# A written order for each engine's queue, from chunk 2 of a fused attention and two-layer MoE kernel on

## The chip, the cores and the metric

The kernel runs on 1 core of one Trainium2 chip. The metric is device time in microseconds of one execution, here the median of several runs. TensorE, VectorE (DVE), ScalarE (ACT), GpSimd (POOL) and SyncE (SP, which issues nearly all loads and stores) each work through a queue of their own in order, and wait for each other by semaphores.

## The reference

Three layers follow one another. Everything is float32 on the chip.

```
# 1. delta-rule attention, 4 batches x 8 heads, 768 positions, head size 48
for t in range(S):
    y[t]  = q[t] @ state
    v_old = state.T @ k_n[t]
    state = state + beta[t] * outer(k_n[t], v[t] - v_old)
# 2. dense layer on the 3072 tokens x 384
h = x @ w_in;  x = silu(h) @ w_out          # 384 -> 2048 -> 384
# 3. eight experts, one chosen per token, tokens with x @ w_skip <= 0 pass through
e = argmax(x @ w_gate);  out = x + p[e] * (relu(x @ w1[e]) @ w2[e])
```

## The kernel before, in words

The 768 positions are cut into 12 chunks (NCH) of 64. In a chunk the recurrence is written with matrices: the Gram matrix of the chunk's keys (grams) gives a triangular matrix that has to be inverted (`inverse(c)`, some 80 small steps in a row on VectorE, most of them the pairs of lines 457 and 462), and with the inverse and the state St the outputs and the next state follow. One chunk of one batch goes through these stages (`chain(c, b)`):

- `pre`: GpSimd scales the values into vp (line 512) and the inverse into T (line 518); ScalarE copies the state into SU (line 527).
- `ks` (line 534): state times keys, subtracted from vp by VectorE (line 542).
- `u1` (line 547): first half of the solution; ScalarE copies it into U (line 552), GpSimd into SU (line 556).
- `g21u` (line 564), subtracted on VectorE; `u2` (line 573), copied by ScalarE into SU (line 578).
- `supd` (line 591): the new state, copied into St by VectorE (line 594).
- `yout` (line 605): the output; ScalarE writes its high part into x (line 614) and VectorE the low part. After the last batch a small DMA on SyncE moves rows inside x (line 620).

Chunks are prepared two ahead in eight slots: SyncE loads kq (`load_qk`, line 140, four buffers) and PQ (line 1025), ScalarE spreads the keys into KtB (`prep_t`, line 295), TensorE makes the grams (`prep_g`, line 300), ScalarE takes the diagonal blocks into Gd (line 376) and the lower ones into G21 (line 342), and VectorE masks the gram into PQ (`mask_q`, line 354). The inverse reads Gd by two transposes (line 398) and ends with a scaling and a transpose into Xb (lines 477 and 479). Gd, the inverse's buffers and Xb exist once, for chunk 2 and later ones.

Layer 2 of chunk c has 256 tokens and goes in 16 SiLU tiles (MF) of 128 hidden units. `l1(c, m)` (line 631) is nine matmuls into a PSUM tile hp: weights and activations are split into a high and a low part, and three products of 3 matmuls each are added. ScalarE applies SiLU twice, into gh and gf (lines 636, 637), GpSimd takes the difference gl (line 638), and `l2` (line 648) is nine matmuls that add into xp. After tile 15, `x2out` copies xp (line 662 on VectorE, line 657 on ScalarE), six float32 matmuls (line 668, twelve records in the trace) transpose it and make the router's logits, ScalarE and VectorE take them out (lines 670, 673), SyncE stores rows of x2 and out (lines 678, 679). `route1` and `route2` choose the experts on VectorE (lines 693 to 756) and GpSimd scatters the token numbers (line 760); line 756 writes these numbers into ids. A matmul of float32 operands makes two records in the trace, one of l1 or l2 makes one.

What sets the order: the program gives each instruction a priority, by the `rank` under which it was written (a chunk's step, and within it CHAIN, PREP, INV, CONV, MOE in this order). A planner that knows an estimate of each duration goes through a simulated time and appends to each engine's queue the ready instruction of the best rank. Buffers are given out in the same order. So the queues hold chain, inverse, preparation and SiLU layer mixed as the planner saw them become ready. In the queues of before the SiLU layer of chunk c-1 runs beside the attention of chunk c and part of c+1.

The start of the program converts the dense layer's weights, on VectorE, up to 139 us. After the layer of chunk 11 come its routing, the gathers and the eight experts.

Of the kernel before, what the change touches and what calls it, by code (L numbers as in the profile page):

```python
# [8 lines left out]
F32 = mybir.dt.float32  # L9
# [7 lines left out]
AX = mybir.AxisListType  # L17
PSUM = bass.MemoryType.PSUM
DRAM = bass.MemoryType.DRAM


@with_exitstack
def kernel(
# [22 lines left out]

    nc = tc.nc
    NCH, B, _, _, NP, CH = qk.shape  # L50
    D = ki.shape[-1]
    H, S = 2 * NP, NCH * CH
# [234 lines left out]
    def slot(c, b):  # L287
        return slots[c * B + b]
# [78 lines left out]
        spread(j, kq_t[c, b][:, 1])  # L367

    def prep_g(c, b):
        j = slot(c, b)  # L370
        g = ps_g.tile([128, NP, 128], F32, tag="g", name="g")
        for p in range(NP):
            gram(j, p, g[:, p, :], kq_t[c, b][:, :, p, :])
        for blk in range(2):
            sl = slice(64 * blk, 64 * blk + 64)
            nc.scalar.activation(
                out=Gd[sl, b * NP:(b + 1) * NP, :], in_=g[sl, :, CH + 32 * blk:CH + 32 * blk + 32], func=AF.Copy
            )
        lower(j, g[:, :, CH:])
        mask_q(j, g[:, :, 0:CH])  # L380
# [7 lines left out]
    def inverse(c):  # L388

        steps = []  # L390
        V = nc.vector
        nw = ar.tile([128, 5, 32], F32, tag="nw", name="nw")
        Gi, X = (Gi1, X1) if c == 1 else ([Gi0[:, 0:16], Gi0[:, 16:32]], X0)
        tmp = tmps[c == 1]
        w = [nw[:, z, :] for z in range(5)]

        def fwd(y0):
            return V.transpose(
                out=Gi[y0 // 16],
                in_=Gd[:, :, y0:y0 + 16].rearrange("p i y -> p y i")[:, :, None, :].to_broadcast([128, 16, 2, 16]),  # L400
            )

        steps.append(lambda: fwd(0))
        steps.append(lambda: fwd(16))

        i0, i1 = w[0].bitcast(I32), w[1].bitcast(I32)

        def norm():
            if c < 2:
                nc.scalar.activation(out=X, in_=Xi, func=AF.Copy)  # L410
            else:
                nc.gpsimd.tensor_copy(out=X, in_=Xi)
            for z in range(2):
                i = V.tensor_scalar(
                    out=w[0][:, 16 * z:16 * z + 16],
                    in0=Gi[z].rearrange("p a b -> p (a b)")[:, 16 * z:512:33], scalar1=1e-30, scalar2=None,
                    op0=ALU.max,
                )
            return i

        steps.append(norm)
        steps.append(lambda: V.tensor_scalar(
            out=i1, in0=i0, scalar1=1, scalar2=None, op0=ALU.logical_shift_right))
        steps.append(lambda: V.tensor_scalar(
            out=i1, in0=i1, scalar1=-1.0, scalar2=float(0x5F3759DF), op0=ALU.mult, op1=ALU.add))
        for _ in range(3):
            steps.append(lambda: V.tensor_tensor(out=w[2], in0=w[1], in1=w[1], op=ALU.mult))
            steps.append(lambda: V.scalar_tensor_tensor(
                out=w[2], in0=w[2], scalar=-0.5, in1=w[0], op0=ALU.mult, op1=ALU.mult))
            steps.append(lambda: V.scalar_tensor_tensor(  # L430
                out=w[1], in0=w[2], scalar=1.5, in1=w[1], op0=ALU.add, op1=ALU.mult))
        steps.append(lambda: V.tensor_tensor(out=w[2], in0=w[1], in1=w[0], op=ALU.mult))
        steps.append(lambda: V.tensor_scalar(out=w[2], in0=w[2], scalar1=1e-6, scalar2=None, op0=ALU.add))
        steps.append(lambda: V.reciprocal(out=w[3], in_=w[2]))
        steps.append(lambda: V.tensor_tensor(out=w[4], in0=w[3], in1=bet[:, c, :], op=ALU.mult))
        steps.append(lambda: V.tensor_tensor(out=w[4], in0=w[4], in1=w[3], op=ALU.mult))

        E = nc.gpsimd if c == 1 else V
        pre = E is nc.gpsimd

        def scale(y0):
            return (nc.gpsimd if c else V).tensor_tensor(
                out=Gi[y0 // 16], in0=Gi[y0 // 16],
                in1=w[4][:, y0:y0 + 16, None].to_broadcast([128, 16, 32]), op=ALU.mult,
            )

        def flat(j, r0, r1):
            f = (r0 - j // 2) * j
            return tmp[:, f:f + (r1 - r0) * j].rearrange("p (n j) -> p n j", j=j)

        def mul(j, r0, r1):
            n = r1 - r0
            a = X[:, r0:r1, j:j + 1].to_broadcast([128, n, j])
            b = Gi[j // 16][:, j % 16:j % 16 + 1, 0:j].to_broadcast([128, n, j])
            if pre:
                return E.tensor_tensor(out=flat(j, r0, r1), in0=a, in1=b, op=ALU.mult)
            return V.scalar_tensor_tensor(  # L457
                out=flat(j, r0, r1), in0=a, scalar=w[4][:, j:j + 1], in1=b, op0=ALU.mult, op1=ALU.mult
            )

        def sub(j, r0, r1):
            return E.tensor_tensor(  # L462
                out=X[:, r0:r1, 0:j], in0=X[:, r0:r1, 0:j], in1=flat(j, r0, r1), op=ALU.subtract
            )

        if pre:
            steps.append(lambda: scale(16))
        for j in range(31, 0, -1):
            if pre and j == 28:
                steps.append(lambda: scale(0))  # L470
            r0 = j // 2
            for f in (mul, sub):
                steps.append(lambda f=f, j=j, r0=r0: f(j, r0, 16))

        def last():
            V.transpose(out=nat, in_=w[2])
            V.tensor_tensor(
                out=X, in0=X, in1=w[4][:, None, :].to_broadcast([128, 16, 32]), op=ALU.mult)
            return V.transpose(out=Xb.rearrange("p i (r s) -> p r s i", s=2), in_=X)

        pace["inv", c] = [i for i in (f() for f in steps) if i is not None]
        return last

# [23 lines left out]
        return dict(vp=vp, T=T, U=U, su=su, pr=ru[:, 0], pu=ru[:, 1])  # L507

    def pre(c, b):
        g = gr[c, b] = tiles(c, b)  # L510
        vp, T, su = g["vp"], g["T"], g["su"]
        nc.gpsimd.tensor_tensor(
            out=vp,
            in0=v_t[c, b // 2][:, b % 2 * NP:(b % 2 + 1) * NP],
            in1=nat[:, b * NP:(b + 1) * NP][:, :, None].to_broadcast([128, NP, D]),
            op=ALU.mult,
        )
        nc.gpsimd.tensor_tensor(
            out=T,
            in0=Xb[:, b * NP:(b + 1) * NP, None, :].to_broadcast([128, NP, 2, 32]),  # L520
            in1=m2[:, None, :, None].to_broadcast([128, NP, 2, 32]),
            op=ALU.mult,
        )
        if c:
            with tc.issue_after(seen["hi", 0].ins) if c == 1 else ExitStack():
                for h, _, n, r0, r1 in feat:
                    nc.scalar.activation(out=su[r0:r0 + n, h, :, 0:D], in_=St[r1:r1 + n, b], func=AF.Copy)  # L527

    def ks(c, b):
        g = gr[c, b]  # L530
# [65 lines left out]
    def yout(c, b):  # L596
        g = gr[c, b]
        j = slot(c, b)
        if c or b % 2 == 0:
            py = ps_c.tile([128, NP, CH], F32, tag="y", name="py", bufs=1)  # L600
        else:
            py = ps_g.tile([128, NP, CH], F32, tag="g", name="py")
# [400 lines left out]
            tc.cur_priority = self.old  # L1003

    marks = {}
    js1 = []
    gates = deque()
    todo = deque(range(NCH * B))
# [2 lines left out]
    def prep():  # L1011
        while free and todo:
# [3 lines left out]
            with rank(c - 1, PREP):  # L1016
                if c == 0 and b == B - 1:
                    prep_0()
                elif c:
# [9 lines left out]
                    elif b == B - 1:  # L1029
                        js1[:] = [slot(c, i) for i in range(B)]  # L1030
                        grams(c, js1, 1)
            if b == B - 1 and c:
                with rank(c - 1, INV) if c > 1 else rank(0, INV):
                    last_of[c] = inverse(c)
            if b == B - 1 and not c:
# [2 lines left out]
    def chain(c, b):  # L1038
        with rank(c, CHAIN):
            with rank(c, CHAIN) if c else rank(-2, 5 + b):  # L1040
                if b % 2 == 0:
                    load_v(c, b // 2, nc.sync)
                if c < NCH - 1:
                    load_k(c, b, nc.sync)
            pre(c, b)
        if b == B - 1 and 0 < c < NCH - 1:
            with rank(c, INV):
                last_of.pop(c + 1)()
        with rank(c, CHAIN):
            with tc.issue_after(seen["yout", 0].ins) if c == 1 else ExitStack():  # L1050
                ks(c, b)
            u1(c, b)
            g21u(c, b)
            u2(c, b)
            if c:
                supd(c, b)
            yout(c, b)
            if not c:
                supd(c, b)
        free.append(slots[c * B + b])  # L1060
# [20 lines left out]
    def moe(c):  # L1081
        for m in range(MF + 1):
            moe_part(c, m)

    with rank(-2, 0):
        for z in (1, 0):
# [60 lines left out]
    for m in range(MF + 1):  # L1147
        moe_part(0, m)
    prep()
    for c in range(1, NCH):  # L1150
        for b in range(B):
            chain(c, b)
            prep()
        if c > 1:
            moe(c - 1)
    tc.cur_priority = (NCH + 2) * STEP + MOE
    st_att.close()
    open_e1()
# [135 lines left out]
```

## Time and profile before

| | us |
|---|---|
| median of 3 runs | 990.09 |
| lowest and highest run | 985.07, 994.03 |
| the profiled execution | 981.84 |
| its span, first to last instruction | 980.0 |

| engine | busy us in the span | share |
|---|---|---|
| TensorE matmul | 866.6 | 88% |
| VectorE | 607.8 | 62% |
| ScalarE | 476.1 | 49% |
| GpSimd | 398.0 | 41% |

Busy is the union of the instructions' times on an engine; for matmuls the end is modelled and holds the drain, under which the next matmul runs. The granted clock says at what share of 2.4 GHz TensorE was let run. Stretches below are cut at the first l1 matmul of a layer: the layer of chunk 1 begins at 148.7 us, the following ones at 224.1, 280.8, 346.0, 415.2, 481.4, 542.0, 597.3, 654.9 and 708.9, and that of chunk 11 at 758.0.

### The profile page before, as it was taken

How to read it: one execution, taken by the hardware profiler on the slowest of the kernel's cores; microseconds unless marked ns; L12 is line 12 of the kernel's file. 1: busy time of each engine (PE TensorE's matmuls, PEld its weight loads, DVE VectorE, ACT ScalarE, POOL GpSimd, SP SyncE). 2: the span in 40 equal slices, each digit the busy share in tenths (PEclk: the TensorE clock that was granted, in tenths of full speed). 3: DMA queues.
4: the chain of work that ended last, by engine and by line, in shares of the span. 5: the costliest groups of instructions: out<-in, count | busy, mean ns of one | idle time of the engine just before them, and what ended most of it. 6: DMA issues, size and time to landing. Idle time of an engine off the chain costs nothing. (4 is left out here: it accounts for less than half of the span.)

```text
span 980.0 us, 21718 instructions
## 1 busy us (share of the span) xinstructions
PE 866.6 (88%) x8177; PEld 827.5 (84%) x8177; DVE 607.8 (62%) x1776; ACT 476.1 (49%) x1290; POOL 398.0 (41%) x581
## 2 busy tenths in 40 slices
PE   7188998899996997978999999999999975999994
PEld 7177888889996987968999999899998964999994
DVE  5997999778624857357576954748523114776541
ACT  4167883465462553453464555445255342565520
POOL 4588663333322332422433342343345433435411
PEclk8567899998997997998999999999999996999998
DMA  9952221232222222132141222201018103866400
GB/s 306 401 172 73 69 77 43 59 87 77 69 65 77 63 71 83 31 108 58 46 123 30 86 73 74 82 12 47 9 35 267 34 17 107 283 202 204 151 20 23
DMA packets 64899, 95.83 MB, mean 98 GB/s; under 512 B 9290, under 2 KB 46232, under 8 KB 64784
## 3 DMA queue, kind: packets, MB, share of 16 engines
q1 hardware_dynamic: 61968, 89.69, 29.6%
q0 software_dynamic: 2816, 4.65, 1.7%
q8 instruction: 66, 1.08, 0.5%
q14 instruction: 49, 0.40, 0.1%
HBM read 80.79 MB, written 12.91 MB: 96 GB/s over the span
## 5 line engine op out<-in xcount | busy, mean ns | idle before, releaser
L631 PE MATMUL hp<-x,w 128*128 128x256 f32 x1728 | 263.6, 289 | 0.8 <-ACT gf L637 0.5
L638 POOL TENSOR_TENSOR gl<-gf,gh 128x256 fp32r<-128x256 f32 x192 | 147.8, 770 | 263.4 <-ACT gf L637 226.0
L631 PEld LDWEIGHTS hp<-x,w 128*128 128x128 f32 x1728 | 230.7, 194 | 3.1 <-ACT gf L637 0.7
L648 PE MATMUL xp<-gh,w 128*128 128x256 f32 x1152 | 184.2, 293 | 10.7 <-ACT gh L636 10.2
L648 PEld LDWEIGHTS xp<-gh,w 128*128 128x128 f32 x1152 | 154.5, 192 | 14.0 <-ACT gh L636 10.8
L636 ACT ACTIVATE gh<-hp 128x256 fp32r<-128x256 f32 x192 | 73.3, 382 | 176.9 <-PE hp L631 173.6
L457 DVE SCALAR_TENSOR_TENSOR tmp<-X,nw,Gi 128x126 f32<-128x126 f32 (+22 forms) x341 | 125.7, 369 | 9.3
L462 DVE TENSOR_TENSOR X<-X,tmp 128x126 f32<-128x126 f32 (+22 forms) x341 | 109.2, 320 | 8.8
L648 PE MATMUL xp<-gl,w 128*128 128x256 f32 x576 | 107.4, 293 | 3.4 <-POOL gl L638 3.3
L648 PEld LDWEIGHTS xp<-gl,w 128*128 128x128 f32 x576 | 83.5, 192 | 5.9 <-POOL gl L638 4.4
L527 ACT ACTIVATE SU<-St 32x192 f32<-32x192 f32 (+1 forms) x176 | 63.6, 361 | 46.5 <-PE py L605 22.4
L637 ACT ACTIVATE gf<-hp 128x256 f32<-128x256 f32 x192 | 72.9, 379 | 18.9 <-POOL gl L638 18.1
L300 PE MATMUL g<-kq,KtB 128*128 128x128 f32 (+1 forms) x384 | 66.1, 310 | 16.0 <-issue 10.2
L300 PEld LDWEIGHTS g<-kq,KtB 128*128 128x128 f32 x384 | 55.9, 215 | 18.4 <-issue 12.9
L881 PE MATMUL ehp<-exh,ew 128*128 128x256 f32 x384 | 66.8, 284 | 0.0
L814 ACT ACTIVATE ew<-eraw 128x768 fp32r<-128x768 f32 x64 | 53.3, 842 | 21.6 <-PE yp L903 15.4
L385 DVE TENSOR_TENSOR vp<-vp,ru 64x192 f32<-64x192 f32 x48 | 16.9, 358 | 75.0 <-PE ru L564 45.9
L816 DVE TENSOR_TENSOR ew<-eraw,ew 128x768 fp32r<-128x768 f32 x48 | 49.4, 1037 | 19.0 <-ACT ew L814 18.9
L354 DVE COPY_PREDICATED PQ<-mU,g 128x512 f32<-128x512 uint8 x44 | 31.9, 729 | 46.5 <-DMA PQ<-in_qp_dram 23.0
L881 PEld LDWEIGHTS ehp<-exh,ew 128*128 128x128 f32 x384 | 58.7, 191 | 0.0
L903 PE MATMUL yp<-ew,egh 128*128 128x384 f32 x256 | 57.4, 341 | 1.2 <-ACT egh L887 1.2
L534 PE MATMUL ru<-St,KtB 128*128 128x48 f32 x352 | 50.8, 279 | 5.2 <-DVE St L594 5.1
(170 smaller groups left out, 1458.5 us busy)
## 6 DMA issues: line engine op xcount, KB each, us to landing
eraw<-in_w_dram SPq DMA_DIRECT2D x64, 384.0 KB
kq<-in_qk_dram SPq DMA_DIRECT2D x44, 256.0 KB
PQ<-in_qp_dram SPq DMA_DIRECT2D x44, 256.0 KB
ki<-in_ki_dram SPq DMA_DIRECT2D x44, 192.0 KB
raw<-in_w_out_dram SPq DMA_DIRECT2D x16, 384.0 KB
raw<-in_w_in_dram SPq DMA_DIRECT2D x16, 384.0 KB
x2s<-xs SPq DMA_DIRECT2D x24, 197.0 KB
v<-in_v_dram SPq DMA_DIRECT2D x24, 192.0 KB
```

The source lines that it names most:

```text
L300: return nc.tensor.matmul(out, lhsT=KtB[j][:, p].rearrange("p k h t -> p (k h t)"), rhs=rhs, start=True, stop=True, skip_group_check=True,)
L457: return V.scalar_tensor_tensor(out=flat(j, r0, r1), in0=a, scalar=w[4][:, j:j + 1], in1=b, op0=ALU.mult, op1=ALU.mult)
L462: return E.tensor_tensor(out=X[:, r0:r1, 0:j], in0=X[:, r0:r1, 0:j], in1=flat(j, r0, r1), op=ALU.subtract)
L527: nc.scalar.activation(out=su[r0:r0 + n, h, :, 0:D], in_=St[r1:r1 + n, b], func=AF.Copy)
L631: nc.tensor.matmul(hp, lhsT=win[m][:, z, kk], rhs=x[:, kk, :], start=(n == 0), stop=(n == 8))
L636: nc.scalar.activation(out=gh, in_=hp, func=AF.Silu)
L637: nc.scalar.activation(out=gf, in_=hp, func=AF.Silu)
L638: (nc.vector if c == 0 and m in () else nc.gpsimd).tensor_tensor(out=gl, in0=gf, in1=gh.bitcast(F32), op=ALU.subtract)
L648: nc.tensor.matmul(mm[c][jj // 2][:, jj % 2], lhsT=wout[m][:, z, jj], rhs=g_, start=(m == 0 and g_ is gh and z == 0 and jj % 2 == 0), stop ...
L814: nc.scalar.activation(out=t[:, 0], in_=r, func=AF.Copy)
L881: i = nc.tensor.matmul(hp, lhsT=a[:, z, kk, fs], rhs=x[:, kk, :], start=(n == 0), stop=(n == 8))
L903: i = nc.tensor.matmul(ex["y", e][a], lhsT=g_[:, ts], rhs=b[:, z, m % mp], start=(m == 0 and n == 0), stop=(m == ME - 1 and n == 2),)
```

## The change

For chunks 2 to 11 the ranks no longer decide. A wrapper InOrder stands for the object that issues instructions; while it is on, it ties each instruction to the one written before it on the same engine. This is an edge for the planner alone: no semaphore and no instruction comes of it. A function `period(c)` writes the order: 17 steps m, each with l1 of tile m and l2 of tile m-1 of chunk c-1, one stage of the attention of chunk c for two batches (batches 0 and 1 in steps 0 to 4, 2 and 3 in steps 5 to 9), and steps of the inverse of chunk c+1 on VectorE, two at the step's beginning, one after each batch, two at its end. Loads, the routing of chunk c-2 and the preparation of chunk c+2 have fixed steps. `prep_g` and `pre` are cut in two so that their halves can be placed; in a period the odd batches' grams go into a PSUM tile of ps_c and the odd outputs into ps_g. Chunks 0 and 1, the preparation of chunk 3 and all after chunk 11's attention stay with the ranks.

```diff
+class InOrder:
...
+            def call(*args, **kw):
+                traced = own.tc.nc.cur_bb.bb.instructions
+                n = len(traced)
+                r = f(*args, **kw)
+                for i in traced[n:] if own.on else ():
+                    if i.engine in own.last:
+                        own.tc.add_manual_dep(
+                            i, own.last[i.engine],
+                            mybir.DependencyInfo(mybir.DependencyClass.NoSync, mybir.DependencyReason.DATA),
+                            reason="in order",
+                        )
+                    own.last[i.engine] = i.name
+                return r
...
-    nc = tc.nc
+    nc = InOrder(tc)
...
+    def prep_m(c, b):
         j = slot(c, b)
-        g = ps_g.tile([128, NP, 128], F32, tag="g", name="g")
+        if nc.on and b % 2:
+            g = ps_c.tile([128, NP, 128], F32, tag="c", name="g", bufs=2)
+        else:
+            g = ps_g.tile([128, NP, 128], F32, tag="g", name="g")
         for p in range(NP):
             gram(j, p, g[:, p, :], kq_t[c, b][:, :, p, :])
...
+        if nc.on:
+            return steps + [last]
         pace["inv", c] = [i for i in (f() for f in steps) if i is not None]
...
-        if c or b % 2 == 0:
+        if b % 2 == 0 or c and not nc.on:
             py = ps_c.tile([128, NP, CH], F32, tag="y", name="py", bufs=1)
...
-            if b == B - 1 and c:
+            if b == B - 1 and 0 < c < FIRST + 1:
...
+    def period(c):
+        more = c + 2 < NCH
+        inv = deque(inverse(c + 1) if c + 1 < NCH else ())
+        if c == FIRST:
+            for i in range(2):
+                load_v(c, i, nc.sync)
+                load_k(c, i, nc.sync)
+            for b in (0, 1):
+                pre_s(c, b, SU[b % 2])
+                pre_t(c, b)
+
+        def step(n):
+            for _ in range(n):
+                if len(inv) > 1:
+                    inv.popleft()()
+
+        def stage(f, bs):
+            for b in bs:
+                f(c, b)
+                step(1)
+
+        A, Z = (0, 1), (2, 3)
+        for m in range(MF + 1):
+            step(2)
+            if m < MF:
+                l1(c - 1, m)
+            if m:
+                l2(c - 1, m - 1)
+            if m < 4:
+                stage((ks, u1, g21u, u2)[m], A)
+            elif m == 4 or m == 9:
+                bs = A if m == 4 else Z
+                for f in (supd, yout):
+                    stage(f, bs)
+                for b in bs:
+                    if more:
+                        j = slots[(c + 2) * B + b] = slot(c, b)
+                        nc.sync.dma_start(out=PQ[j], in_=qp[c + 2, b])
+                    if m == 4 and c < NCH - 1:
+                        load_k(c, b + 2, nc.sync)
+                    if m == 9 and c < NCH - 2:
+                        load_k(c + 1, b - 2, nc.sync)
+                if m == 4:
+                    for b in Z:
+                        pre_t(c, b)
+            elif m < 9:
+                stage((ks, u1, g21u, u2)[m - 5], Z)
+            if m == 0:
+                finish(c - 2, 0)
+            elif m in (1, 3):
+                finish(c - 2, (m + 1) // 2)
+            if m in (0, 3) and more:
+                for b in ((0, 1) if m == 0 else (2, 3)):
+                    load_qk(c + 2, b, nc.sync)
+            if m in (1, 6) and c + 1 < NCH:
+                load_v(c + 1, m // 6, nc.sync)
+            if m in (5, 6):
+                pre_s(c, m - 3, SU[m % 2 ^ 1])
+            if m in (11, 12) and c + 1 < NCH:
+                pre_s(c + 1, m - 11, SU[m - 11])
+            if more:
+                if 6 <= m < 10:
+                    slots[(c + 2) * B + m - 6] = slot(c, m - 6)
+                    prep_t(c + 2, m - 6)
+                if m in (10, 13):
+                    b = (m - 10) // 3 * 2
+                    prep_m(c + 2, b)
+                    prep_m(c + 2, b + 1)
+                    prep_e(c + 2, b)
+                if m in (11, 14):
+                    prep_e(c + 2, (m - 11) // 3 * 2 + 1)
+            step(2)
+            if m == MF - 2:
+                while len(inv) > 1:
+                    step(1)
+            if m == MF - 1 and inv:
+                inv.popleft()()
+            if m == MF and c + 1 < NCH:
+                for b in A:
+                    pre_t(c + 1, b)
...
-    for c in range(1, NCH):
-        for b in range(B):
-            chain(c, b)
-            prep()
-        if c > 1:
-            moe(c - 1)
+    for b in range(B):
+        chain(1, b)
+        prep()
+    nc.on = True
+    for c in range(FIRST, NCH):
+        with rank(c, CHAIN):
+            period(c)
+    nc.on = False
```

## Rows read from the trace of the kernel before

**Rows 1.** Windows: length, busy us (x) of PE, PEld, DVE, ACT, POOL; clock; DMA share; GB/s.

```profile
148.70:224.10 75.40, 67.98 (x653) 63.84 (x651) 59.59 (x179) 34.46 (x104) 25.30 (x43) 0.93 0.21 61
...
280.80:346.00 65.20, 56.68 (x584) 54.38 (x582) 39.84 (x129) 32.05 (x98) 20.24 (x31) 0.92 0.26 75
346.00:415.20 69.20, 61.09 (x612) 57.78 (x611) 38.62 (x130) 31.15 (x93) 22.67 (x38) 0.93 0.21 63
415.20:481.40 66.20, 57.31 (x584) 54.76 (x582) 36.33 (x128) 29.74 (x90) 20.31 (x34) 0.92 0.25 66
481.40:542.00 60.60, 58.34 (x617) 55.16 (x616) 43.26 (x138) 32.31 (x98) 22.76 (x38) 1.00 0.27 76
542.00:597.30 55.30, 54.94 (x574) 52.08 (x574) 33.09 (x120) 28.68 (x84) 22.66 (x37) 1.00 0.24 70
597.30:654.90 57.60, 55.49 (x585) 52.97 (x585) 39.16 (x129) 28.41 (x86) 20.38 (x33) 1.00 0.23 67
654.90:708.90 54.00, 53.35 (x561) 50.52 (x559) 36.85 (x124) 24.35 (x74) 19.95 (x32) 1.00 0.10 31
708.90:758.00 49.10, 47.01 (x452) 44.70 (x452) 14.90 (x39) 26.00 (x66) 22.93 (x30) 1.00 0.47 150
```

**Rows 2.** Timeline: waits that a load ended; start, length, engine, idle before.

```profile
306.90 0.84 ACT L295 ACTIVATE KtB<-kq 64x256 f32<-64x256 f32 x2 [11.97 <-DMA kq<-in_qk_dram]
...
370.23 0.72 DVE L354 COPY_PREDICATED PQ<-mU,g 128x512 f32<-128x512 uint8 x1 [11.19 <-DMA PQ<-in_qp_dram]
...
442.67 0.72 DVE L354 COPY_PREDICATED PQ<-mU,g 128x512 f32<-128x512 uint8 x1 [10.84 <-DMA PQ<-in_qp_dram]
```

**Rows 3.** SyncE's waits (total, times, longest us), and one PQ issue from the timeline.

```profile
SPq L140 <- PE g L300: 158.9, 21, 22.3
...
433.96 0.38 SPq L1025 DMA_DIRECT2D PQ<-in_qp_dram  x1
```

**Rows 4.** VectorE's waits, from 148.7 to 758 us; total, times, longest us.

```profile
DVE ids L756 <- DMA lst<-ids,si: 25.0, 9, 4.3
```

**Rows 5.** Timeline of TensorE's groups; start us, length us, instructions merged.

```profile
505.03 0.66 PE L573 MATMUL ru<-vp,T 64*64 64x48 f32 x8
...
511.78 1.23 PE L631 MATMUL hp<-x,w 128*128 128x256 f32 x9
...
513.91 1.23 PE L631 MATMUL hp<-x,w 128*128 128x256 f32 x9
...
213.25 0.99 PE L534 MATMUL ru<-St,KtB 128*128 128x48 f32 x8
...
214.83 0.69 PE L605 MATMUL py<-PQ,SU 128*64 128x64 f32 x16
...
289.91 0.56 PE L591 MATMUL ru<-SU,ki 128*48 128x48 f32 x16
...
159.31 1.06 PE L300 MATMUL g<-kq,KtB 128*128 128x128 f32 x8
...
761.97 1.58 PE L668 MATMUL xr<-iwg,xt 128*128 128x138 f32 x12
```

**Rows 6.** Groups by line on VectorE, 481.4 to 542 us; busy us, mean ns.

```profile
L398 DVE STREAM_TRANSPOSE Gi<-Gd 128x512 f32<-128x512 f32 x4 | 4.2, 1101 | 1.8 <-ACT Gd L376 1.8
...
L662 DVE COPY xt<-xp 128x512 f32<-128x512 f32 x1 | 0.7, 677 | 0.0
```

**Rows 7.** Timeline of VectorE: one subtraction of the inverse with GpSimd idle.

```profile
519.56 0.28 DVE L462 TENSOR_TENSOR X<-X,tmp 128x110 f32<-128x110 f32 x1
```

**Rows 8.** Timeline of the end of inverse 2 and the first u1 of chunk 2.

```profile
169.82 0.68 DVE L462 TENSOR_TENSOR X<-X,tmp 128x16 f32<-128x16 f32 x1
...
175.55 0.21 DVE L756 TENSOR_SCALAR ids<-idb 128x1 int32<-128x1 f32 x2 [4.00 <-DMA lst<-ids,si]
...
176.40 1.04 DVE L479 STREAM_TRANSPOSE Xb<-X 128x512 f32<-128x512 f32 x1
...
178.20 1.51 PE L547 MATMUL ru<-vp,T 64*64 64x48 f32 x16 [2.70 <-POOL T L518]
```

More of the change, by code (lines that the diff above doesn't have):

```diff
@@ L19, with __init__, __getattr__ @@
 DRAM = bass.MemoryType.DRAM
+class InOrder:
+    def __init__(self, tc):
+        self.tc, self.on, self.last = tc, False, {}
+        for name in ("tensor", "vector", "scalar", "gpsimd", "sync"):
+            setattr(self, name, self.Engine(self, getattr(tc.nc, name)))
+    def __getattr__(self, name):
+        return getattr(self.tc.nc, name)
+    class Engine:
+        def __init__(self, owner, eng):
+            self.owner, self.eng = owner, eng
+        def __getattr__(self, name):
+            f, own = getattr(self.eng, name), self.owner
+            def call(*args, **kw):
[11 more added lines that the diff above has]
+                return r
+            return call if callable(f) else f
 @with_exitstack
@@ L369, in prep_g, with prep_e @@
     def prep_g(c, b):
+        prep_m(c, b)
+        prep_e(c, b)
+    gp = {}
+    def prep_m(c, b):
         j = slot(c, b)
-        g = ps_g.tile([128, NP, 128], F32, tag="g", name="g")
+        if nc.on and b % 2:
+            g = ps_c.tile([128, NP, 128], F32, tag="c", name="g", bufs=2)
+        else:
+            g = ps_g.tile([128, NP, 128], F32, tag="g", name="g")
         for p in range(NP):
             gram(j, p, g[:, p, :], kq_t[c, b][:, :, p, :])
+        gp[c, b] = g
+    def prep_e(c, b):
+        j = slot(c, b)
+        g = gp.pop((c, b))
         for blk in range(2):
@@ L509, in pre, with pre_t @@
     def pre(c, b):
+        pre_t(c, b)
+        if c:
+            pre_s(c, b, gr[c, b]["su"])
+    def pre_t(c, b):
         g = gr[c, b] = tiles(c, b)
-        vp, T, su = g["vp"], g["T"], g["su"]
+        vp, T = g["vp"], g["T"]
         nc.gpsimd.tensor_tensor(
@@ L523, in pre, with pre_s @@
         )
[L524 to L527, printed above, removed]
+    def pre_s(c, b, su):
+        with tc.issue_after(seen["hi", 0].ins) if c == 1 else ExitStack():
+            for h, _, n, r0, r1 in feat:
+                nc.scalar.activation(out=su[r0:r0 + n, h, :, 0:D], in_=St[r1:r1 + n, b], func=AF.Copy)
     def ks(c, b):
@@ L1005 @@
     marks = {}
+    FIRST = 2
     js1 = []
@@ L1045, in chain @@
             pre(c, b)
-        if b == B - 1 and 0 < c < NCH - 1:
+        if b == B - 1 and c == 1:
             with rank(c, INV):
@@ L1083, in moe @@
             moe_part(c, m)
+    def period(c):
[39 more added lines that the diff above has]
+                    for b in Z:
+                        pre_t(c, b)
+            elif m < 9:
[33 more added lines that the diff above has]
+                    pre_t(c + 1, b)
```

## The prediction

> **What bounds the kernel now.** I read the windows cut at the first matmul of each SiLU layer first [rows 1]. From 481.4 us on, where the clock is granted in full, TensorE is busy 47 to 58 us of stretches of 49 to 61 us: 96 to 99% of all but the last. There the kernel is bound by TensorE, and no order can give much back. Before that it is another picture. The stretches from 280.8, 346.0 and 415.2 last 65.2, 69.2 and 66.2 us, with TensorE idle for 65.2-56.7 = 8.5, 8.1 and 8.9 us, and a granted clock of 0.92 to 0.93. As the clock has two levels, 0.92 of 65.2 us is 10.4 us at 1.2 GHz. Each has one pause, and behind it the clock is low. The stretch from 148.7 is the worst: 75.4 us, idle 7.4, clock 0.93.
>
> What are the three pauses? The timeline names them [rows 2]: once ScalarE stands 12.0 us for a kq load, twice VectorE stands 11 us for a PQ load at the masking of line 354, and everything queued behind it stands too (the SU copies, the SiLU evictions, the subtractions on which TensorE waits). The load at 442.67 had been issued at 433.96, 8.7 us earlier [rows 3]: too late, because SyncE's queue is in order and had stood for releases of kq buffers, 159 us in all, up to 22.3 at once. VectorE has a second foreign wait: the ids tile of line 756, which waits for a scatter, 25.0 us in 9 waits, up to 4.3 [rows 4]. The chain that ended last reaches back only through the experts' last store, so it says nothing of this part; the sum is made over stretches.
>
> **The change, part by part.** I call "period c" the SiLU layer of chunk c-1 with the attention of chunk c.
>
> Work removed or added: none that is an instruction. The written edges bind one engine to its own order and issue nothing. Odd gram and output tiles swap PSUM banks at equal number. So the TensorE work of a full period stays. It is 590 matmul records: 16 SiLU tiles at 2.13 us from one l1 to the next, 34.1 [rows 5]; for each of 4 batches one group of ks, three of u1, g21u, u2, one of yout, supd and grams, 0.99 + 3x0.66 + 0.69 + 0.56 + 1.06 = 5.28, 21.1 in all; the router 1.58. That is 56.8 as an upper bound, since a length holds the drain of the last matmul, under which the next group starts: nine l1 matmuls last 1.23, yet eighteen take 2.13, so 0.165 of a group is drain. Without it the seven groups of a batch and the router give 34.1 + 4x4.12 + 1.4 = 52.0, the lower bound. Whole stretches scale to 54.94x590/574 = 56.5, small waits included [rows 1]. I take 55.0.
>
> Head of a period (m = 0), a wait that is added. The router's matmuls come in order behind ks, and want the copy of line 662, which on VectorE stands behind two transposes of the inverse, two subtractions and two small steps: 2x1.10 + 4x0.28 + 0.68 = 4.0, and 0.4 of hand-offs by estimate [rows 6, 7]. TensorE has l1 and ks beside it, 1.07 + 2x0.85 = 2.8, and stands 1.6. Queued behind it are l1 and l2 of tile 1; nothing else is late. At the other end the last gl is 0.4 late, as no l1 covers it. A period is 55.0 + 1.6 + 0.4 = 57.0.
>
> The stage hand-offs cost nothing: between a stage and the next lie one l1 and l2 (2.13) against one ScalarE or VectorE eviction for each of two batches, each shorter than the 0.68 of line 662's larger copy, and between them one inverse step of 0.28 [rows 6, 7]. The inverse is covered by slack: VectorE is busy 43.3 us of the 60.6 from 481.4, ScalarE 32.3, GpSimd 22.8 [rows 1]. If that cover is gone, it is the second rival.
>
> Loads on SyncE. kq for chunk c+2 is issued at m = 0 and 3 for use at m = 6 to 9, PQ at m = 4 and 9 for masking at m = 10 to 14. The shortest lead is that of the second PQ pair: four tiles and two grams, some 12 us, less 2 for the x copies ahead of it in the queue, so 10 against the 8.7 seen. Its release is the yout just before, ki's the supd; the long kq waits go, since a kq buffer was freed a whole period earlier. So the pauses of 8.5, 8.1 and 8.9 go, with the low clock behind them, and what is late next is nothing but the head. The ids writes move behind their own si, a period after the scatter that frees them: their 25 us go too. GpSimd keeps gl first in every tile; T and vp for the next pair follow it at m = 4 and 16, a whole tile or more before use.
>
> Start of period 2, the part that costs. Before, the l1 of chunk 1's layer ran freely while TensorE's attention waited for the inverse of chunk 2: it ended at about 170.5, Xb followed only behind an ids wait of 4.0, and u1 came at 178.2 [rows 8]. In the written order u1 stands at m = 1, and the router of m = 0 stands behind the first transposes of inverse 3, which must wait until inverse 2 has let go of the buffers. From 170.5: the last scaling and transpose 1.8, the head's 4.0, router 1.4: m = 1 begins at 177.7. What VectorE did for chunks 0 and 2 in the meantime is now queued behind (routing of chunk 0, one transpose, a copy; about 5 us), so at best 172.6. I take 175. Until then TensorE has one l1, ks and the grams of chunk 3, and will stand for some 20 us, after which the clock is low: up to 10.4/2 = 5.2 us lost, I take 3.5. Period 3 then begins at 175 + (57.0-5.8) + 3.5 = 229.7, against 224.1 before.
>
> **Sum.** Periods 3 to 9: 7x57.0 = 399.0. Period 10 has no grams (3.9 less): 53.1. Period 11 has no supd and no inverse (1.5 and 1.6 less): 50.0; the stretch of the same work before was 49.1. The layer of chunk 11 begins at 229.7 + 399.0 + 53.1 + 50.0 = 731.8, before at 758.0: 26.2 less. Behind that nothing changes: expert loads start when the last yout has freed its tiles, now some 14 us ahead of that layer and ahead of need by far more. The profiled execution took 981.84 us (span 980.0); 955.6 follows. The median of the runs shown is 8.2 us above that execution, and I put the saving on the median: 990.1 - 26.2 = 964. The saving lies in the first five layers: periods 3 to 7 took 317.9 us and will take 285; periods 8 to 11 took 216.0 and will take 217.
>
> **Rivals.** (a) More: the work of a period is nearer its lower end and the pause at the start is filled. With periods of 55.2, and period 3 at 222: 222 + 386.4 + 51.3 + 48.2 = 708, so 940. For it: 54.0 and 55.3 have been reached [rows 1]. Against it: these held fewer records.
> (b) The slower side: an in-order hand-off is late in most tiles. Place: ten hand-offs a period, where the planner used to slip another matmul in and TensorE must now stand. It decides from 26.2/10 = 2.6 us a period, that is 0.26 for each hand-off beyond its 2.13 of cover. At 5 us a period the time is 1014; at 2 it is 984. For it: before, VectorE stood 10.8 us for one late tile and held up all that was queued [rows 2]. Against it: two evictions of under 0.68 have 2.13 of cover.
> (c) VectorE becomes the bound. A bare subtraction took 0.28, while one of a seventh of the columns took 0.68 beside a GpSimd operation [rows 7, 8]. If GpSimd's 22.8 us were all added to VectorE's 43.3, a period would be 66 and the time about 1045. Against it: the 43.3 were measured with these collisions in them, at 60.6 us.
> The Trainium skill (SBUF — State Buffer, "SBUF: two separate sides") says that VectorE and GpSimd lock one shared port pair, so that an operation with two SBUF inputs waits out a GpSimd operation that reads SBUF. By that rule (c) has its mechanism; these rows agree with it, but they show it as paid already.
> (d) The change doesn't do what it says: late loads only move (the second PQ pair has 1.3 us to spare), or the order written is much that of before. Then the pauses stay: about 988.
>
> **How the numbers follow.** Chances: the forecast (952 to 976) 0.58; (a) 0.12; (b) mild, 976 to 992, 0.10, and 1000 or more 0.12; (d) 0.06; (c) 0.02. A measurement tells about 1% from no change, here 9.9 us. Faster by more: the forecast, (a) and the near third of mild (b), 0.73. Within 1%: the rest of mild (b), and (d), 0.13. Slower: 0.14. The range reaches from (a)'s price to the end of mild (b), 941 to 992, and leaves out what lies above, 0.14, and a little below.
>
> **What would show it.** Ten even stretches of some 57 us from the second layer on, clock 1.00, no wait of ScalarE or VectorE for a kq or PQ load, no ids wait; one stand of 1 to 2 us at the router in each period; one pause of about 20 us near 155 to 175, with a low clock behind. Wrong if TensorE stands at u1, g21u or u2 in every tile, if VectorE is over 95% busy, if the pause at the start is over 40 us, or if the masking still waits for PQ.

## The result and the profile after

The changed kernel took 952.75 us (median of 4 runs, 952.39 to 953.63), the one before 990.93 in the runs beside it (4 runs, 985.07 to 994.03): a ratio of 0.962, 95% interval 0.958 to 0.967. In the comparisons made later the kernel before stood at 984.0 to 985.1 (medians of 7 to 13 runs), so the saving is 31 to 38 us, depending on which runs of before one takes. The two profiled executions, 981.84 and 952.64 us, differ by 29.2, and these 29.2 can be placed.

In the changed kernel every instruction issued through the wrapper carries the wrapper's line, L43, so its rows are read by tiles. The windows, cut at the first l1 matmul of each layer, with the columns of [rows 1]:

```profile
149.00:223.70 74.70, 58.47 (x609) 56.65 (x608) 56.90 (x176) 31.56 (x95) 21.50 (x36) 0.89 0.19 59
223.70:281.10 57.40, 55.94 (x592) 54.19 (x591) 41.96 (x130) 30.38 (x91) 21.32 (x35) 0.97 0.25 76
281.10:337.20 56.10, 54.72 (x593) 52.77 (x592) 41.09 (x130) 30.39 (x91) 21.36 (x35) 1.00 0.28 78
337.20:394.50 57.30, 56.01 (x592) 54.27 (x591) 41.19 (x129) 30.38 (x91) 21.35 (x35) 0.97 0.25 76
...
507.90:565.20 57.30, 56.01 (x592) 54.27 (x591) 41.19 (x130) 30.39 (x91) 21.35 (x35) 0.97 0.24 76
...
622.40:674.80 52.40, 51.02 (x561) 49.17 (x560) 37.52 (x125) 23.00 (x67) 21.65 (x36) 1.00 0.13 36
674.80:729.40 54.60, 51.57 (x485) 49.33 (x484) 14.68 (x45) 26.10 (x67) 23.40 (x34) 0.94 0.33 103
729.40:765.00 35.60, 35.13 (x297) 34.88 (x296) 3.62 (x22) 11.61 (x34) 15.34 (x20) 1.00 0.25 74
```

Seven periods in a row, 223.7 to 622.4, last 56.1 to 57.4 us with the same 592 or 593 records; before, they ran from 55.3 to 69.2 [rows 1]. Stretch by stretch, after less before: layer 1 -0.7, layer 2 +0.7, layers 3 to 6 -9.1, -11.9, -8.9 and -4.5, layers 7 to 9 +2.0, -0.4 and -1.6, layer 10 +5.5; layer 1 begins 0.3 later and what lies behind layer 10 is 0.6 shorter. The sum is -29.2. All of the gain lies in four layers; the last full ones give none, and the last period costs.

The waits of the changed kernel from 223 to 765 us (total, times, longest us):

```profile
PE xr L43 <- DVE xt L43: 11.7, 9, 1.5
PE xp L43 <- ACT gh L43: 1.5, 1, 1.5
...
DVE ids L43 <- DMA lst<-ids,si: 4.2, 1, 4.2
...
ACT ew L43 <- DMA eraw<-in_w_dram: 4.1, 3, 1.8
...
SPq L43 <- DVE xs L43: 173.2, 9, 19.8
SPq L43 <- DVE X L43: 107.2, 8, 17.7
```

No wait for a kq or PQ load is left, where before three of 11 to 12 us stood [rows 2]; the ids write waits once. TensorE has one kind of stand in every layer, the router's, nine times 1.2 to 1.5 us, and one of 1.5 us for a SiLU in layer 10. SyncE's queue still stands: over all its rows from 149 to 760 us the waits are 474 us, before 515. Nobody is late for it.

The head of period 3 and the start of period 2, on the timeline (start, length, engine, idle before):

```profile
170.11 3.10 PE L43 MATMUL xr<-iwg,xt 128*128 128x138 f32 x12 [16.23 <-DVE xt L43]
172.84 2.08 PE L43 MATMUL hp<-x,w 128*128 128x256 f32 x9
...
223.65 2.02 DVE L43 STREAM_TRANSPOSE Gi<-Gd 128x512 f32<-128x512 f32 x2
223.68 1.23 PE L43 MATMUL hp<-x,w 128*128 128x256 f32 x9
...
224.75 1.88 PE L43 MATMUL ru<-St,KtB 128*128 128x48 f32 x16
...
227.26 0.67 DVE L43 COPY xt<-xp 128x512 f32<-128x512 f32 x1
...
228.09 2.08 PE L43 MATMUL xr<-iwg,xt 128*128 128x138 f32 x12 [1.46 <-DVE xt L43]
...
229.83 2.29 PE L43 MATMUL hp<-x,w 128*128 128x256 f32 x9
```

The copy of line 662 comes 3.6 us after the first transpose, behind what the prediction listed, and TensorE has run out of l1 and ks by then. The next l1 then takes 2.29 us instead of 1.23: the clock, to which I come back at the end.

### The profile page after: what moved, and what is told of

It reads as the page before. It is cut to its first block, busy times and chain, and to the rows that moved or that the text cites. A ratio compares the mean times of both kernels' runs of the same rounds, so it can differ in the third digit from the quotient of the medians.

```text
span 950.8 us, 21622 instructions
## 1 busy us (share of the span) xinstructions
PE 845.5 (89%) x8177; PEld 816.1 (86%) x8177; DVE 630.0 (66%) x1776; ACT 474.3 (50%) x1290; POOL 389.1 (41%) x581
## 5 line engine op out<-in xcount | busy, mean ns | idle before, releaser
L43 POOL TENSOR_TENSOR gl<-gf,gh 128x256 fp32r<-128x256 f32 x192 | 145.6, 758 | 338.9 <-ACT gf L43 312.2
L43 PE MATMUL hp<-x,w 128*128 128x256 f32 x1728 | 258.3, 295 | 1.6 <-ACT gf L43 1.3
L43 PEld LDWEIGHTS hp<-x,w 128*128 128x128 f32 x1728 | 226.1, 195 | 6.9 <-ACT gf L43 1.5
L43 PE MATMUL xp<-gh,w 128*128 128x256 f32 x1152 | 170.5, 284 | 2.4 <-ACT gh L43 2.0
L43 DVE SCALAR_TENSOR_TENSOR tmp<-X,nw,Gi 128x126 f32<-128x126 f32 (+22 forms) x341 | 149.7, 439 | 10.6
L43 PEld LDWEIGHTS xp<-gh,w 128*128 128x128 f32 x1152 | 152.9, 191 | 3.1 <-ACT gh L43 2.4
L43 ACT ACTIVATE gh<-hp 128x256 fp32r<-128x256 f32 x192 | 73.2, 381 | 161.7 <-PE hp L43 160.8
L43 DVE TENSOR_TENSOR X<-X,tmp 128x126 f32<-128x126 f32 (+22 forms) x341 | 101.5, 298 | 8.5
L43 PE MATMUL xp<-gl,w 128*128 128x256 f32 x576 | 103.3, 288 | 0.4 <-POOL gl L43 0.3
L43 PEld LDWEIGHTS xp<-gl,w 128*128 128x128 f32 x576 | 82.4, 190 | 1.9 <-POOL gl L43 0.8
L43 ACT ACTIVATE gf<-hp 128x256 f32<-128x256 f32 x192 | 72.7, 379 | 0.9 <-POOL gl L43 0.8
L43 PE MATMUL ehp<-exh,ew 128*128 128x256 f32 x384 | 66.9, 284 | 0.0
L43 ACT ACTIVATE SU<-St 32x192 f32<-32x192 f32 (+1 forms) x176 | 63.6, 361 | 2.7
L43 ACT ACTIVATE ew<-eraw 128x768 fp32r<-128x768 f32 x64 | 53.3, 843 | 21.8 <-PE yp L43 15.5
L43 DVE TENSOR_TENSOR vp<-vp,ru 64x192 f32<-64x192 f32 x92 | 31.9, 350 | 45.5 <-PE ru L43 33.9
L43 DVE TENSOR_TENSOR ew<-eraw,ew 128x768 fp32r<-128x768 f32 x48 | 49.1, 1029 | 18.5 <-ACT ew L43 18.3
L43 PE MATMUL g<-kq,KtB 128*128 128x128 f32 (+1 forms) x384 | 54.0, 291 | 7.9 <-DMA kq<-in_qk_dram 3.7
L43 DVE COPY_PREDICATED PQ<-mU,g 128x512 f32<-128x512 uint8 x44 | 32.3, 738 | 40.0 <-ACT G L43 39.9
L43 PEld LDWEIGHTS ehp<-exh,ew 128*128 128x128 f32 x384 | 58.7, 191 | 0.0
L43 PE MATMUL ru<-vp,T 64*64 64x48 f32 x768 | 56.5, 224 | 2.0 <-DVE vp L43 1.9
L43 PEld LDWEIGHTS g<-kq,KtB 128*128 128x128 f32 x384 | 49.9, 205 | 9.4 <-DVE PQ L43 3.1
L43 PE MATMUL yp<-ew,egh 128*128 128x384 f32 x256 | 57.5, 341 | 0.0
```

The source lines that it names most:

```text
L43: r = f(*args, **kw)
```

## The experiments

Theory 1 says that the gain comes from SyncE's written order: loads are no longer late. Theory 2 says that it comes from the written order of the four compute engines. Theory 3 is in the expectations of e1 and e2 that the gain is the ids writes, which no longer stand for a scatter. After the third run I widened it, and so it is meant below: the period's text, which says where loads, stages and SiLU tiles are issued, does nearly all by the ranks alone, and the edges only guard one hazard, the ids write.

**e1: edges on SyncE alone.**

```diff
 for i in traced[n:] if own.on else ():
+    if i.engine != mybir.EngineType.SP:
+        continue
```

> The written edges bind SyncE's queue alone; the other four engines are filled by the planner from the period's program order. Theory 1 (the saving is that of loads that arrive in time, because SyncE's order is written): 950 to 965 us, no wait of over 2 us for a kq or PQ load, layers 3 to 5 at 55 to 60 us. Theory 2 (the saving is that of the written order on the compute engines): 975 us or more. Theory 3 (the ids writes that stood on VectorE's queue for a scatter): the ids waits come back, about 970.

1053.13 us, ratio 1.065 (1.059 to 1.072). Theory 1 fell: the slowest kernel of all. Its layers 2 to 8 take 68.5 to 71.5 us, and its timeline shows one load made late:

```profile
306.63 2.96 SPq L43 DMA_DIRECT2D x2s<-xs  x1
309.63 3.41 SPq L43 DMA_DIRECT2D out_dram<-xs  x1
313.16 4.21 SPq L43 DMA_DIRECT2D kq<-in_qk_dram  x2
...
325.05 0.84 ACT L43 ACTIVATE KtB<-kq 64x256 f32<-64x256 f32 x2 [14.36 <-DMA kq<-in_qk_dram]
...
326.20 1.00 PE L43 MATMUL xp<-gh,w 128*128 128x256 f32 x3 [11.89 <-ACT gh L43]
```

The loads stand at their written place behind the router's row stores, while ScalarE, unbound, reached the KtB copy at 310.7, before the load was issued at 313.2. In the changed kernel the same stores stand ahead of kq, but ScalarE comes to the copies at their written place: kq is issued at 237.8 and used at 254.5. Here ScalarE waits for kq 115.0 us in 8 waits, and the SiLU behind it stops TensorE.

**e2: edges on all engines but SyncE.**

```diff
+    if i.engine == mybir.EngineType.SP:
+        continue
```

> The edges bind the four compute engines, SyncE's queue is free. Theory 1: load waits come back, with pauses of 5 to 9 us and a low clock behind each, 965 us or more. Theory 2: 950 to 958 us. Theory 3: about 953, as the ids writes stay in their place.

958.27 us, 0.971 (0.966 to 0.976), layers 2 to 8 of 56.6 to 57.8, no wait for kq or PQ. As theory 2 said, if a hair above its 950 to 958; SyncE's edges are worth 5.5 us.

**e3: the whole text, no edge.**

```diff
-                for i in traced[n:] if own.on else ():
+                for i in traced[n:] if False and own.on else ():
```

> The period's text stays, with its PSUM tiles and its place for each step, but no edge binds any queue: the planner may pull anything forward. Theories 1 and 2: much of the saving is lost, 970 to 990 us, with load waits and ids waits back. If it stays at 953, the program order alone made the saving and the edges nothing.

993.52 us (10 runs, 979.26 to 995.05), 1.002 (0.997 to 1.007): nothing is gained. So the edges seem to be everything. But the load waits that I expected back are not there: no wait for kq or PQ. Only the ids wait is back, 41.8 us in 10, on the timeline:

```profile
319.95 0.21 DVE L43 TENSOR_SCALAR ids<-idb 128x1 int32<-128x1 f32 x2 [4.67 <-DMA lst<-ids,si]
...
323.74 0.31 PE L43 MATMUL ru<-vp,T 64*64 64x48 f32 x2 [3.09 <-DVE vp L43]
```

The write of ids (line 756) can be appended to VectorE's queue as soon as idb is there, before the scatter that still reads the tile has ended. The subtraction for u1 stands behind it, and TensorE behind that.

**e4: the kernel before, once more** (one run; 986.88 us).

> The kernel before once more, unchanged, for its spread: the median of its runs lies 9 us above the execution profiled first. Theory 1: the load waits depend on when a transfer lands, so that pauses come and go; this execution takes 985 to 994 us and shows one or two more pauses of 5 to 9 us than the three of the first. If the number of pauses is the same, the spread has another cause.

The three pauses are the same, 8.7, 8.1 and 8.9 us; the 5 us more lie in the clock (layer 4 at 0.88 against 0.93, 70.9 us against 69.2) and the experts. Between these two executions, the number of pauses did not change; one run can't say more about the spread of before.

**e5: no edges, an ids tile for each chunk; e6: the same tile in the kernel before.**

```diff
-        ids = rot.tile([128, 2], I32, tag="ids", name="ids")
+        ids = rot.tile([128, 2], I32, tag="ids", name="ids", bufs=NCH)
```

> The kernel without edges, and ids given twelve buffers in place of two, so that the write of line 756 of before can be put anywhere without waiting for a scatter. Theory 3 (in that kernel the 42 us of ids waits on VectorE made u1 late, TensorE stood and its clock fell): 955 to 968 us, layers 3 to 9 at 55 to 58 us, no low clock in them. Theory 2 (the written order at large on the compute engines): 980 us or more, stands at u1 as before.

> The kernel before with twelve ids buffers, nothing else. Theory 1b (before, the three pauses of 8 to 9 us for kq and PQ loads, with the low clock behind them, are the loss): the pauses stay, 980 to 988 us. Theory 3: the ids waits were the loss, 955 to 970 us.

e5 took 940.89 us, 0.956 (0.951 to 0.960): one buffer size is worth some 50 us in that program (52.6 by the medians, where the ten runs of e3 spread over 16), which without a single edge beats the changed kernel and the 955 to 968 that I expected. Its layers, from the windows:

```profile
218.70:280.70 62.00, 62.00 (x590) 59.16 (x591) 43.65 (x136) 32.07 (x97) 21.27 (x35) 0.88 0.26 75
...
445.70:500.80 55.10, 55.10 (x592) 53.00 (x591) 40.09 (x127) 30.26 (x91) 21.68 (x36) 1.00 0.29 79
```

A full layer holds no idle time at all. In e6 the same edit is worth only 5.6 us: 978.52, 0.994 (0.992 to 0.997); the waits for PQ (25.3 us in 5) and kq (18.0 in 5) stay. So the ids waits were not the loss of before, which had been e6's rival (955 to 970). Theory 2 fell as well, as edges on the compute engines aren't needed for the gain, and theory 3 stands in its wider form: the text cures the late loads, and edges or a larger ids tile cure the other. Which part of the text it is, no run tried alone.

**e7: the router's copies first.** The two copies of lines 657 and 662 are written ahead of the period's first inverse steps; all edges stay.

```diff
         for m in range(MF + 1):
+            if m == 0:
+                x2copy(c - 2)
             step(2)
```

> The changed kernel with the two copies of the router's input written first in a period, ahead of the inverse's transposes. By the prediction's head of a period the stand of 1.3 us goes in ten periods, with it the low clock of 3.4 us that followed it in five or six of them (1.2 us each), and at the start of period 2 the router and tile 1 run before the pause, some 4 us: 13 + 6 + 4 = 23 us less, about 930. Rival: the stand only moves, to u1 behind the late subtraction, 945 to 955.

931.76 us (930.06 to 935.95), 0.945 (0.941 to 0.949): 21 us from moving two copies, the fastest kernel of this study. A full layer and its head:

```profile
445.00:499.60 54.60, 54.50 (x592) 52.64 (x591) 41.10 (x129) 30.52 (x91) 21.35 (x35) 1.00 0.27 80
```

```profile
281.15 1.23 PE L43 MATMUL hp<-x,w 128*128 128x256 f32 x9
281.23 0.69 DVE L43 COPY xt<-xp 128x512 f32<-128x512 f32 x1
...
283.93 1.65 PE L43 MATMUL xr<-iwg,xt 128*128 128x138 f32 x12
285.67 1.33 PE L43 MATMUL hp<-x,w 128*128 128x256 f32 x9
```

The stand of 1.46 and the slow l1 behind it are both gone. The layers 2 to 10 take 485.0 us, 20.7 less than in the changed kernel; of that 4.1 are given back ahead of them and behind them in the profiled execution. What is left is the start: one wait of 14.1 us in layer 1.

**e8: the expert's first splits later**, on ScalarE bound behind the last SiLU of layer 10.

```diff
-                *((seen["x2"].ins, seen[n].ins) if e == 1 else ()),
+                *((seen["x2"].ins, seen[n].ins) if e == 1 else (seen["gf"].ins, None) if e == 0 else ()),
```

> The changed kernel with the split of expert 0's weights on ScalarE bound behind the last SiLU of the layer of chunk 10. If period 11 is 4.6 us longer than forecast because three of these splits stand at the head of ScalarE's queue for their loads: period 11 at 50 us and 947 to 949 us. Rival: the splits now collide with the layer of chunk 11, 952 to 954.

955.73 us, 0.970 (0.966 to 0.974), so 3 us slower than without it. The expected 947 to 949 was missed, and the rival (952 to 954) is nearer. Layer 10 is 49.3 us, as predicted for it, but layer 11 is 42.9 instead of 35.6: the splits now stand ahead of that layer's router and SiLU. The cost moved and grew.

**e9: before with e6's tile, and PQ loaded ahead of kq.**

```diff
+                        nc.sync.dma_start(out=PQ[j], in_=qp[c, b])
                         load_qk(c, b, nc.sync)
-                        nc.sync.dma_start(out=PQ[j], in_=qp[c, b])
```

> The kernel before with twelve ids buffers, and in the preparation the PQ load written ahead of the kq load of the same batch, so that on SyncE's queue it doesn't stand behind that kq load's wait for a buffer. Theory 1b (the pauses of before are PQ and kq loads that stand in SyncE's queue): VectorE's 25 us of PQ waits mostly go, the layer with the largest pause (75 us) falls to 55 to 60, kq waits stay: 960 to 970 us. Rival (the loads are late because of traffic, not of their place in the queue): 975 to 980, PQ waits as before.

1004.84 us, 1.019 (1.014 to 1.024): slower, 26 us above e6, with more waits of both kinds (PQ 35.2 us in 6, up to 12.9; kq 21.4 in 6). My expectation failed: the place of one load in its pair isn't what makes it late.

**e10: e7 with periods from chunk 3 on and e6's tile; e11: e7 with that tile and no edges.**

```diff
-    FIRST = 2
+    FIRST = 3
```

> The copy-first kernel with the written order begun at chunk 3 in place of 2 and twelve ids buffers: chunk 2's attention and the layer of chunk 1 are left to the planner. By the prediction's term for the start of period 2, the pause of 14 us with its low clock goes from the layer of chunk 1 (75 us, to 66 to 70), while period 3 gets a smaller one: 918 to 926 us. Rival: the pause moves to period 3 whole, since inverse 4 is then waited for, 930 us or more.

> The copy-first kernel with twelve ids buffers and no edge at all. Theory 3 (once no instruction without inputs can be pulled in front of the others, and the copy is early, edges add nothing): 930 to 941 us, full stretches at 54.6 to 55.2. Theory 2 (the edges have a worth of their own): 950 us or more, with stands at the stages.

e10: 934.87 us, 0.951 (0.948 to 0.954). The first layer is 5.7 us shorter than in e7, but layer 2 at a clock of 0.92 is 4.6 longer, and each full layer takes 55.2 instead of 54.6. It missed its 918 to 926. e11: 942.97, 0.960 (0.956 to 0.964), between the 930 to 941 of theory 3 and the 950 of theory 2. Beside e7 the edges are worth some 11 us, 4.3 by the two profiled executions, as far as the larger ids tile, by which e11 differs too, does nothing. The difference has no single place: layer 2 is 10.2 longer without them (64.8 us, clock 0.84), the start before it 12.8 shorter, each full layer 0.4 to 0.7 longer, layer 9 3.7. That the full layers take their work and nothing else by the text alone is as theory 3 had it.

**e12: before without the store of line 679.** Two of a layer's four row stores are left out, and with them the rows of out that no expert writes. TensorE's order up to the experts is that of before.

```diff
-            nc.sync.dma_start(out=ov, in_=xs[:, 0:DM])
```

> The kernel before without the store of out's rows on line 679 (two of a layer's four row stores; the rows of out that no expert writes are left out). TensorE's order up to the experts is that of before. If the late kq and PQ loads of before come from the traffic of the row stores issued just ahead of them, their waits halve: the pauses of 8 us in the layers 3, 4 and 5 go to 4 or less, ScalarE's and VectorE's waits for kq and PQ loads fall from some 43 us in 10 (the kernel before with its own ids tile per chunk) to 20 or less, and the time is 960 to 972. If they come from SyncE's queue, which stands for a release, the waits and the pauses stay and the time is within 1% of before.

955.91 us, 0.972 (0.967 to 0.977), a little below the range given for this case. The waits for kq and PQ loads fell less than expected, from 38.5 us in 10 (before, 149 to 765 us) to 25.1 in 7, where I had 20 or less. The windows of the three layers with the pauses:

```profile
277.20:339.40 62.20, 57.46 (x584) 55.16 (x582) 40.15 (x129) 32.22 (x98) 20.25 (x33) 0.95 0.25 72
339.40:404.40 65.00, 60.08 (x614) 56.84 (x612) 38.35 (x130) 31.17 (x93) 22.27 (x37) 0.95 0.21 61
404.40:464.90 60.50, 57.95 (x584) 55.38 (x582) 36.66 (x128) 29.61 (x90) 21.09 (x34) 0.94 0.25 66
```

Idle are 4.7, 4.9 and 2.5 us, where 8.5, 8.1 and 8.9 were [rows 1], though SyncE waits for its kq buffers no less than before (178 us from 149 to 760, before 155). So without two of the four row stores about half of the pauses is gone. The three layers give 12.9 of the 25.6 us between the profiled executions of before and e12; the rest is spread, and the ids waits fell too, from 25.0 us to 9.8. On SyncE, ahead of the load that was late at 442.67 [rows 2], before shows:

```profile
423.45 1.65 SPq L679 DMA_DIRECT2D out_dram<-xs  x1
425.20 2.94 SPq L678 DMA_DIRECT2D x2s<-xs  x1
428.24 5.15 SPq L140 DMA_DIRECT2D kq<-in_qk_dram  x1
```

Issuing one kq load takes 5.15 us here and 0.33 in the median of the 29 issued from 149 to 760 us; two more took 3.7 and 3.9. In e12 none takes over 2.4. The Trainium skill (DMA: Bandwidth & Descriptors, "Queues, rings and completion order") says that one issuing engine owns one ring on each DMA engine, whose descriptors are consumed in ring order. By that a load's transfer starts behind those of the stores issued ahead of it; e12 agrees, with the halved pauses, but doesn't tell this from the traffic that the stores make.

## Why the prediction was right, and where not

The direction and the mechanism held: the sum gave -26.2 us on the profiled execution, and it is -29.2. By its steps:

- **Period length** 57.0: 56.1 to 57.4. The 55.0 for the work itself is shown by e7 and e5, where nothing stands: 54.6 and 55.1. The router's stand of 1.6 is 1.2 to 1.5. That the length fits so well is luck in part: I forecast a clock of 1.00, and five of the seven full periods had 0.97, with 1.2 us of low clock (last section) that no term stood for.
- **The three pauses** go, and what is late next is the head, as said. The reason named was one of two. I blamed SyncE's in-order stand for kq buffers [rows 3], and this stand did go (149 to 760 us; the first line is of before, the second of the changed kernel):

```profile
SPq L140 <- PE g L300: 155.0, 20, 22.3
...
SPq L43 <- PE g L43: 1.3, 2, 0.9
```

  SyncE as a whole stands nearly as long (515 and 474 us), now most of all for the router's result. The shortest lead of a PQ load is 10.4 us, for 10 in the forecast:

```profile
265.72 0.53 SPq L43 DMA_DIRECT2D PQ<-in_qp_dram  x1
...
276.12 0.74 DVE L43 COPY_PREDICATED PQ<-mU,g 128x512 f32<-128x512 uint8 x1 [0.52 <-ACT G L43]
```

  But e12 halves the pauses with the kq stand undiminished: the stores ahead in the queue, or their traffic, count as well, and the prediction had nothing for them. They are not gone from the changed kernel, where eight of 32 kq issues take 3.4 to 5.0 us and no load is late. That the period's text is the cure, and no edge on SyncE, is shown by e2, e3 and e5; that it is the lead it gives the loads is what these rows suggest, and no run has changed the lead alone.
- **The ids write** got no price. It has two: 5.6 us in before (e6), and some 50 in a program with the same text and no edges (e3 against e5). Here lies most of what the compute engines' edges do, and I had listed it as a by-product.
- **Start of period 2.** m=1 began at 172.84 (forecast 175, at best 172.6), after a pause of 16.2 us (some 20). Period 3 began at 223.7 instead of 229.7, the largest miss of the sum. I had put 3.5 us of low clock behind m=1; the windows of the changed kernel show nearly all of it ahead of that point:

```profile
157.50:170.10 12.60, 0.00 (x0) 0.02 (x1) 10.54 (x32) 0.00 (x0) 2.42 (x5) 0.50 0.00 0
170.10:174.50 4.40, 4.39 (x20) 4.40 (x21) 0.85 (x5) 0.98 (x2) 0.47 (x1) 0.50 0.04 7
174.50:223.70 49.20, 49.20 (x548) 47.55 (x548) 37.74 (x116) 28.47 (x86) 18.52 (x30) 1.00 0.29 88
```

- **Period 10** 53.1: 52.4. **Period 11** 50.0: 54.6, the one term too low. The timeline of the changed kernel names the cause, three splits of expert weights in ScalarE's queue ahead of a SiLU:

```profile
716.49 0.84 ACT L43 ACTIVATE ew<-eraw 128x768 fp32r<-128x768 f32 x1 [1.79 <-DMA eraw<-in_w_dram]
...
719.33 0.85 ACT L43 ACTIVATE ew<-eraw 128x768 fp32r<-128x768 f32 x1 [1.44 <-DMA eraw<-in_w_dram]
...
721.00 0.84 ACT L43 ACTIVATE ew<-eraw 128x768 fp32r<-128x768 f32 x1 [0.83 <-DMA eraw<-in_w_dram]
...
722.17 0.97 PE L43 MATMUL xp<-gh,w 128*128 128x256 f32 x6 [1.46 <-ACT gh L43]
```

  I said that the expert loads come earlier and "ahead of need by far more", and didn't ask what ScalarE's queue does with what they trigger. In e8 layer 10 is 49.3 without them, so they are most of the miss: of the 5.3 us between the two kernels 1.7 are TensorE's idle time, and the rest is mostly low clock, two stretches of 3.4 us at 0.50, the first of them behind the router's stand and not behind a split. e8 also shows that the splits can't simply be put off.
- **The layer of chunk 11** began at 729.4 instead of 731.8, and behind it nothing changed (0.6 us), as said. The sum came within 3 us because its two largest misses, -6.0 at period 3 and +4.6 in period 11, nearly cancel; that is luck.
- **From the profile to the median** I added 8.2 us, the distance of before's median from its profiled execution. The changed kernel has no such distance (952.75 and 952.64), and later runs of before stood 2 to 3 us above its own. So 964 was too high by this step more than by the sum's 3 us.

The rivals: (b) has no sign, since TensorE waits for no eviction of a stage. (c) neither: VectorE is busy 41 to 42 us of a full period. (d) is excluded by the waits. (a) is what e7 reaches, a period at its lower end.

Open: the other half of the pauses of before (e12 leaves 4.7, 4.9 and 2.5 us), the queue's stand or the stores that remain; whether the stores act by their place in the queue or by their traffic; and why full layers take 54.9 to 55.3 us in the three programs with period text and the larger ids tile (e5, e10, e11), and 54.6 in e7 without it.

## What to carry to other kernels

When an order is written out by hand, ask first which few places it repairs, and try these alone: here, with the period's text in place, one tile's buffer count did more without any edge than the edges did (940.9 against 952.8 us). In the kernel before, the same tile gave 5.6 us, so the text was needed too. Look then at the head of the written period: a copy that feeds the next matmul belongs ahead of the fillers, and moving two of them gave 21 us more on top of the change's 31 to 38. Loads want a place by what is queued ahead of them, row stores here, and not only by when their buffer is free.

## What I had not expected of the hardware

A stand of 1.2 to 1.5 us was enough to lower TensorE's clock. In six of nine periods the router's stand was followed by 3.4 us at 0.50, that is 1.2 of 2.4 GHz, although TensorE had worked at the full clock up to the stand; one more such stretch followed the stand of 1.46 us for a SiLU in layer 10. The windows of the changed kernel behind the stand of period 3:

```profile
229.20:232.60 3.40, 3.40 (x18) 3.40 (x17) 1.86 (x13) 1.29 (x4) 0.00 (x0) 0.50 0.06 12
...
232.60:236.00 3.40, 3.40 (x36) 3.21 (x36) 3.14 (x15) 1.05 (x4) 2.09 (x5) 1.00 0.14 46
```

The first 3.4 us hold 18 records and the next 36, in part smaller ones; nine l1 records took 2.29 us in the first stretch, and 1.23 ahead of the stand. Full periods with it take 57.2 to 57.4 us, the two without it 56.1, and those of e7, without any stand, 54.6: the low clock costs 1.2 us beside the 1.3 to 1.5 of the stand itself. It isn't the length alone: the stands of periods 4 and 5 were both 1.29 us, and only the second was followed by it. The second surprise is the 5.15 us that SyncE needed to issue a load behind row stores.
